# Six raw buffers for the first half slices of weights, and another order of the first loads

## The chip, the cores and the metric

The kernel runs on one core of one Trainium2 chip. The metric is the device time of one execution in microseconds; lower is better. Times of whole runs are medians; what is said of single instructions comes from one execution taken by the hardware profiler.

## What is computed

Windowed attention with block summaries, then two MLPs. For each head, a query sees the keys within 15 positions (`window` 16) and one summary per block of 32 keys: the largest key, component by component, paired with the mean of the values.

```python
k_sum = k.reshape(B, H, nb, block, D).max(axis=3)
v_sum = v.reshape(B, H, nb, block, D).mean(axis=3)
scores_l = scale * q @ k^T            # only where |i - j| < window
scores_s = scale * q @ k_sum^T + log(block)
a = softmax(concat(scores_l, scores_s))
x = a @ concat(v, v_sum)              # -> 1536 tokens x 512
h = maximum(x @ w_in1, 0); x = (h * h) @ w_out1
h = x @ w_in2; g = P(h) / (Q(h) + 1e-6); out = g @ w_out2
```

Batch 2, 8 heads, 768 positions, 64 components per head; the MLPs go from 512 to 2048 and back. The weights lie in memory as 64-bit floating point numbers; everything else is float32.

## The kernel before

The hidden dimension of the MLPs is cut into slices of 128; a slice of weights has two halves, one of `w_in` (half 0) and one of `w_out` (half 1). Half slice number k belongs to slice k // 2. Its raw 64-bit words are loaded by `w_load` (0.52 MB, lines 103 to 113) into one of three raw buffers with the tag `stage`; then three steps decode it. `w_top` (T, ScalarE, line 120) and `w_dec` (D, VectorE, lines 130 and 131) make a float32 of the two words; `w_put` (W) splits it into a high part (`wh`, ScalarE, line 144) and the rest (`wl`, GpSimd, line 145). The MLP matmuls use both: `l1` (line 532) makes the hidden values of a slice, `l2` (line 619) adds them to the output. In pass 0 the first five slices are applied to blocks of 256 tokens, between pieces of the attention that makes these tokens; passes 1 to 3 do the rest in blocks of 512.

Raw buffers come free when `w_dec` has read them. So `w_next(1)` (lines 739 to 744), the step that decodes half slice k, issues the load of half slice k + NL, where NL is the number of w loads in the list LOADS, 3. All loads go out from one queue, SP's.

The attention works on pairs d of heads and 256 queries; p is the pair of heads. In front of everything, a list LOADS gives the order of the first loads: k0 to k3 keys of a pair of heads, q0 and q1 the queries of the first 256 positions in two halves of the heads, Q1 the queries of the next 256 positions (two DMAs into `acc`), v0 to v3 values for the sums, n0 to n3 the windows of values (ten DMAs, line 318), w0 to w2 half slices. Then a list START gives, step by step, the work of the first 30 us; its instructions stay in the written order on each engine. The steps that matter here: `P`, `R` rearrange keys; `t` transposes keys (PE, line 333), `q` transposes queries (`d_t`, PE, line 397); `z` scales and spreads them (ScalarE, line 405); `s` makes the scores (PE, line 416); `m` adds the mask and finds the largest (VectorE, lines 431 and 435); `e` takes the exponential (ScalarE, line 441); `r` the sums of rows (VectorE); `n` normalises (GpSimd, line 455); `p` transposes the probabilities (PE, line 465); `b`, `f` copy them; `o` multiplies them with the values (PE, line 481); `S` adds four and four rows of the values of a pair of heads (`s_add`, GpSimd, line 286); `V` sums the rest on PE (line 373); `u` and `w` put the sums in place; `T`, `D`, `W` decode w0 to w2. The step q4 reads the queries that Q1 loads; all instructions that follow START on PE, VectorE, ScalarE and GpSimd are queued behind its last one on that engine (`tc.issue_after`), up to a point in the loop.

The work behind START is ordered by a planner that knows estimated times; the order of SP's queue behind the first loads is also its choice. `acc` (128 x 6144) is the output of pass 0, in six groups of 1024 columns, one for each block of 256 tokens; until they are written, groups 4 and 5 hold raw queries.

Of the kernel before, what the change touches and what calls it, by code (L numbers as in the profile page):

```python
# [13 lines left out]
I32 = mybir.dt.int32  # L14
# [2 lines left out]


LOADS = (
    "k0 k1 q0 k2 q1 k3 v0 v1 v3 Q1 v2 w0 n1 n0 n3 n2 w1 w2"  # L20
)
START = (
# [4 lines left out]
)  # L27
# [3 lines left out]
def tile_window_attention_moe_moe(  # L31
# [15 lines left out]
    NT, DM = out.shape  # L47
    DFF = w_in1.shape[1]
    P = 128
# [4 lines left out]
    KC = DM // P  # L54
# [11 lines left out]
    hp = ctx.enter_context(tc.tile_pool(name="hp", bufs=2))  # L66
# [7 lines left out]
    G = 2 * P  # L74
# [8 lines left out]
    acc = const.tile([P, KC * NT], F32, name="acc")  # L83
# [16 lines left out]
    wraw = {}  # L100
    wtop = [t.bitcast(I32) for t in (w_in1, w_out1, w_in2, w_out2)]

    def w_load(n, j):
        m, f = divmod(n, NF)
        r = hp.tile([P, DM, 2], I32, tag="stage", name="wraw", bufs=3)
        if j == 0:
            src = wtop[2 * m].rearrange("(k p) c -> p k c", p=P)[:, :, 2 * f * P:2 * (f + 1) * P]
            nc.sync.dma_start(out=r.rearrange("p (k f) w -> p k (f w)", k=KC), in_=src)
        else:
            nc.sync.dma_start(  # L110
                out=r.rearrange("p e w -> p (e w)"), in_=wtop[2 * m + 1][f * P:(f + 1) * P, :]
            )
        wraw[n, j] = r
# [82 lines left out]
    def build_consts():  # L196
        make_identity(nc, ident)
        for t in early[4:8]:
            nc.gpsimd.memset(t[VP:KP], 0.0)
        for z in qz:  # L200
            nc.vector.memset(z[0:D, :, 1], 0.0)
            nc.vector.memset(z[D:P, :, 0], 0.0)
        for t in prs:
            nc.vector.memset(t[:, :, HK:], 1e-9)
        m = mk[0:LO, 1, 0:WT]
        nc.vector.memset(m, 0.0)
        nc.gpsimd.affine_select(
            out=m, in_=m, pattern=[[1, WT]], compare_op=ALU.is_ge, fill=NEG, base=-1,
            channel_multiplier=-1,
        )  # L210
        nc.gpsimd.affine_select(
            out=m, in_=m, pattern=[[-1, WT]], compare_op=ALU.is_ge, fill=NEG, base=2 * WIN - 1,
            channel_multiplier=1,
        )
        nc.vector.memset(mk[:, :, WT:], math.log(BLK))
        nc.vector.tensor_copy(mk[LO:P, 1, 0:WT], m)
        m = mk[:, 1:2, 0:WT]
        nc.vector.tensor_copy(mk[:, 0:1, 0:WT], m)
        nc.vector.tensor_copy(mk[:, 2:6, 0:WT], m.to_broadcast([P, 4, WT]))
        nc.vector.memset(mk[:, 0, 0:WIN], NEG)  # L220
        nc.vector.memset(mk[:, 5, WT - WIN:WT], NEG)
        nc.gpsimd.memset(kst[VP:KP], 0.0)
        nc.vector.memset(bw, 1.0 / BLK)
        for sgn, base in ((1, 0), (-1, BLK - 1)):
            nc.gpsimd.affine_select(
                out=bw[:, WT:], in_=bw[:, WT:], pattern=[[-sgn * BLK, NB]],
                compare_op=ALU.is_ge, fill=0.0, base=base - (sgn < 0) * (TR - 1),
                channel_multiplier=sgn * TR,
            )
        nc.vector.memset(bw[:, 0:WT], 0.0)  # L230
# [23 lines left out]
    def k_rel(p, copy):  # L254

        t = early[4 + p][0:KP].rearrange("p (r h d) -> p r h d", r=TR, d=D)
        copy(out=t[0:VP].rearrange("p r h d -> p h r d"), in_=ksrc[p])
        ksrc[p] = t
# [34 lines left out]
    def q_load(g, hs=slice(0, H)):  # L293

        bb, i, _, _ = at(g * 2 * NP)
        for j in range(2):
            x = nc.sync.dma_start(
                out=qr[g % 2][:, j, hs],
                in_=q[bb, hs, (i + j) * P:(i + j + 1) * P].rearrange("h p d -> p h d"),
            )  # L300
            if g > 1:
                late(x)

    def v_load(g, hh, j):


        bb, i, _, _ = at(g * 2 * NP + j)
        t = vn[hh][j]
        t0 = i * P - WIN
        for dst, lo, n in ((t[0:WT, 0], t0, WT), (t[0:WT, 1], t0 + LO, WT)):  # L310
            segs = [(0, lo, n)]
            if lo < 0:
                segs = [(0, 0, -lo), (-lo, 0, n + lo)]
            elif lo + n > S:
                e = lo + n - S
                segs = [(0, lo, n - e), (n - e, S - e, e)]
            for r, s, m in segs:
                nc.sync.dma_start(
                    out=dst[r:r + m].rearrange("s (h d) -> s h d", d=D),
                    in_=v[bb, 4 * hh:4 * hh + 4, s:s + m, :].rearrange("h s d -> s h d"),  # L320
                )
# [16 lines left out]
    def k_lin(p, b, copy):  # L338

        pt = pk[p][b]
        src = pt[:, KE:KE + 4 * KP]
        src = bass.AP(src.tensor, src.offset, [
            list(src.ap[0]), [LO // TR, NWIN], [1, WT // TR], [KP, 4],
        ])
        dst = kt[p][:, :, 0:WT].rearrange("p w (t r) -> p w t r", r=TR)
        copy(out=dst[:, :, :, 4 * b:4 * b + 4], in_=src)
        free(pt)
# [117 lines left out]
    def d_b(d, copy=nc.scalar.copy):  # L467
        pp = ap.tile([HK, 4, 2, LO], F32, tag="pp", name="pp", bufs=2)
        copy(out=pp.rearrange("p c e t -> p (c e t)"), in_=po[d][0:HK])
        free(po[d])  # L470
        po[d] = pp
# [238 lines left out]
    v0 = {}  # L710

    def v_early(p):
# [3 lines left out]
    loads = dict(  # L716
        k=e_load, q=lambda j: q_load(0, hh[j]), Q=q_load, v=v_early,
        n=lambda i: v_load(0, *divmod(i, 2)), w=lambda i: w_load(*divmod(i, 2)),
    )
    for x in LOADS.split():  # L720
        loads[x[0]](int(x[1:]))
    NL = LOADS.count("w")
    build_consts()
    nc.gpsimd.memset(abc[:, 4:5], (1.0 + 1e-6) * 2.0 ** -62)
    nc.gpsimd.memset(abc[:, 5:6], -62.0 * math.log(2.0))
# [1 line left out]
    NW = 4 * NF  # L727
    wq = [0, 0, 0]

    def w_step(lim):  # L730

        if wq[2] < wq[1]:
            w_next(2)
        if wq[1] < wq[0]:
            w_next(1)
        if wq[0] < min(lim, NW):
            w_next(0)

    def w_next(j):
        k = wq[j]  # L740
        (w_top, w_dec, w_put)[j](*divmod(k, 2))
        wq[j] += 1
        if j == 1 and k + NL < NW:
            w_load(*divmod(k + NL, 2))

    def w_cap(ps, c, f):

# [25 lines left out]
    def v_last(h, copy):  # L773
# [5 lines left out]
        P=lambda p: k_rel(p, nc.gpsimd.tensor_copy), t=k_tr,  # L779
        l=lambda p: k_lin(p, 0, act), L=lambda p: k_lin(p, 0, dve),  # L780
        k=lambda p: k_lin(p, 1, dve), K=lambda p: k_lin(p, 1, act),
        c=lambda p: k_put(p, some, dve),
        C=lambda p: k_put(p, rest, dve, False), B=lambda p: k_put(p, rest, act, False), q=d_t, z=d_z, s=d_s, m=d_m, e=d_e,
        r=d_r, n=d_n, p=d_p, b=d_b, f=lambda d: d_b(d, dve), o=d_o, x=d_x, y=d_y,
# [5 lines left out]
    with tc.manual_schedule():  # L790
        for x in START.split():
            fn, n = parts[x[0]], int(x[1:])
# [119 lines left out]
```

## Time and profile before

| | us |
|---|---|
| median of three runs | 631.77 |
| lowest and highest run | 630.13, 632.34 |
| span of the profiled execution, first to last instruction | 629.3 |
| TensorE busy in that span | 606.4 |
| VectorE, ScalarE, GpSimd busy | 405.0, 409.8, 359.9 |

The profile gives the span of the profiled execution, not its time as a run; the median of the runs lies 2.5 us above the span. TensorE (PE) is busy for 96% of the span. PEld is the loading of its stationary operand, which runs beside the matmuls. DVE is VectorE, ACT ScalarE, POOL GpSimd, SP the engine whose queue issues the DMAs. A row of the list of instructions gives the start and the duration in us, the engine and line, the operation, what it writes and reads, a count where neighbours are merged, and in brackets how long the engine stood idle before it and what ended that.

### The profile page before, as it was taken

The numbers are of one execution on the slowest core, as the hardware profiler recorded it, in microseconds if no ns is written. First come the engines' busy times: TensorE is split into PE (matmuls) and PEld (weight loads), VectorE is DVE, ScalarE is ACT, GpSimd is POOL, SyncE is SP. The second block draws the span as 40 slices with busy tenths as digits, with TensorE's granted clock in tenths as the row PEclk, the third lists the DMA queues.
The fourth block names the chain that finished last, engine by engine and source line by source line (L and its number), as shares of the span: only waits on it lengthen the run. The fifth ranks groups of instructions, "written<-read, shape, count | busy, mean of one in ns | idle before, by whom it ended". The sixth has DMA issues, their size and how long they took to land.

```text
span 629.3 us, 9629 instructions
## 1 busy us (share of the span) xinstructions
PE 606.4 (96%) x3492; PEld 518.2 (82%) x3492; DVE 405.0 (64%) x649; ACT 409.8 (65%) x785; POOL 359.9 (57%) x367
## 2 busy tenths in 40 slices
PE   5988899999999999999999999999999999999996
PEld 5777899999998778888888888788888888888885
DVE  7977856555767642111137799987766977776672
ACT  3988767666576433122256898988878788777760
POOL 8649746435668634222276899855545765544441
PEclk9989899999999999999999999999999999999999
DMA  9989951321556530000006532410000100010011
GB/s 220 233 217 246 224 111 38 73 52 59 177 171 196 170 100 1 0 1 0 1 0 201 164 111 95 133 35 0 2 0 2 33 2 0 1 53 15 1 67 67
DMA packets 64142, 51.47 MB, mean 82 GB/s; under 512 B 39776, under 2 KB 56160, under 8 KB 64096
## 3 DMA queue, kind: packets, MB, share of 16 engines
q1 hardware_dynamic: 64096, 50.87, 29.6%
q8 instruction: 27, 0.44, 0.3%
q14 instruction: 19, 0.16, 0.1%
HBM read 47.71 MB, written 3.15 MB: 81 GB/s over the span
## 4 chain that ended last, share of the span: by engine, by line
PE 51%; DVE 7%; POOL 3%; ACT 3%; issue 1%; DVEq 0%; POOLq 0%; ACTq 0%
PE y L619 26%; PE h L532 25%; DVE wdec L131 2%; POOL wl L145 2%; ACT wdec L120 1%; POOL sl L596 1%; DVE h L581 1%; DVE wdec L130 1%; DVE q L578 1%; DVE p L566 1%; DVE p L584 1%; DVE acc L645 1%; DVE p L565 1%; ACT sh L595 1%; ACT wh L144 0%
## 5 line engine op out<-in xcount | busy, mean ns | idle before, releaser
L532 PE MATMUL h<-xh,wh 128*128 128x512 f32 (+1 forms) x444 | 162.5, 366 | 3.7 <-DVE r L562 2.3
L532 PE MATMUL h<-xh,wl 128*128 128x512 f32 (+1 forms) x444 | 161.1, 364 | 2.1 <-POOL wl L145 2.1
L532 PE MATMUL h<-xl,wh 128*128 128x512 f32 (+1 forms) x444 | 161.3, 364 | 0.0
L596 POOL TENSOR_TENSOR sl<-r,sh 128x512 fp32r<-128x512 f32 (+1 forms) x63 | 69.1, 1097 | 105.6 <-ACT sh L595 92.4
L553 POOL TENSOR_TENSOR q<-q,u 128x512 f32<-128x512 f32 x48 | 63.7, 1327 | 76.2 <-ACT q L550 73.2
L145 POOL TENSOR_TENSOR wl<-wdec,wh 128x512 fp32r<-128x512 f32 x64 | 87.2, 1374 | 22.1 <-ACT wh L144 22.1
L532 PEld LDWEIGHTS h<-xh,wh 128*128 128x128 f32 x444 | 84.4, 190 | 17.6 <-DVE r L562 2.5
L532 PEld LDWEIGHTS h<-xh,wl 128*128 128x128 f32 x444 | 84.4, 190 | 15.2 <-POOL wl L145 2.7
L532 PEld LDWEIGHTS h<-xl,wh 128*128 128x128 f32 x444 | 84.6, 191 | 12.5
L562 DVE TENSOR_TENSOR r<-r,h 128x512 f32<-128x512 f32 (+1 forms) x63 | 34.9, 556 | 88.9 <-ACT r L545 88.8
L619 PE MATMUL y<-sh,wh 128*128 128x512 f32 (+1 forms) x252 | 86.1, 345 | 1.2 <-ACT sh L595 1.2
L619 PE MATMUL y<-sh,wl 128*128 128x512 f32 (+1 forms) x252 | 84.7, 339 | 0.0
L619 PE MATMUL y<-sl,wh 128*128 128x512 f32 (+1 forms) x252 | 78.6, 342 | 0.3 <-POOL sl L596 0.3
L596 POOL TENSOR_TENSOR sl<-p,sh 128x512 fp32r<-128x512 f32 x48 | 65.0, 1355 | 20.4 <-ACT sh L595 16.5
L619 PE MATMUL y<-wl,sh 128*128 128x512 f32 x192 | 74.7, 389 | 0.0
L619 PE MATMUL y<-wh,sh 128*128 128x512 f32 x192 | 74.4, 389 | 0.0
L619 PE MATMUL y<-wh,sl 128*128 128x512 f32 x192 | 73.6, 389 | 0.0
L131 DVE SCALAR_TENSOR_TENSOR wdec<-wraw,wdec 128x512 int32<-128x512 int32 x64 | 67.9, 1061 | 1.4
L130 DVE TENSOR_SCALAR wdec<-wdec 128x512 int32<-128x512 int32 x64 | 44.8, 700 | 22.2 <-ACT wdec L120 22.0
L595 ACT CAST sh<-r 128x512 fp32r<-128x512 f32 (+1 forms) x63 | 32.4, 514 | 39.5 <-PE y L619 38.6
L144 ACT CAST wh<-wdec 128x512 fp32r<-128x512 f32 x64 | 39.3, 621 | 28.8 <-DVE wdec L131 26.9
L545 ACT ACTIVATE r<-h 128x512 f32<-128x512 f32 (+1 forms) x63 | 31.0, 493 | 41.3 <-PE h L532 23.6
(94 smaller groups left out, 1106.8 us busy)
## 6 DMA issues: line engine op xcount, KB each, us to landing
wraw<-in_moe_w_in_dram SPq DMA_DIRECT2D x32, 512.0 KB, 4.1
wraw<-in_moe_w_out_dram SPq DMA_DIRECT2D x32, 512.0 KB, 3.4
early<-in_v_dram SPq DMA_DIRECT2D x40, 96.0 KB, 3.3
out_dram<-acc SPq DMA_DIRECT2D x12, 256.0 KB, 2.1
acc<-in_q_dram SPq DMA_DIRECT2D x10, 256.0 KB, 6.1
early<-in_k_dram SPq DMA_DIRECT2D x4, 384.0 KB, 5.4
early<-in_v_dram SPq DMA_DIRECT2D x4, 384.0 KB, 8.6
kst<-in_k_dram SPq DMA_DIRECT2D x8, 192.0 KB, 6.2
```

Source lines behind the costliest of these rows:

```text
L120: x = nc.scalar.activation(out=f32(t), in_=f32(r[:, :, 1]), func=AF.Prelu, scale=2.0 ** -112, alpha=-(2.0 ** 32))
L130: nc.vector.tensor_single_scalar(out=t, in_=t, scalar=3, op=ALU.logical_shift_left)
L131: nc.vector.scalar_tensor_tensor(out=t, in0=low, scalar=29, in1=t, op0=ALU.logical_shift_right, op1=ALU.bitwise_or)
L144: nc.scalar.copy(out=th[:, j], in_=t)
L145: nc.gpsimd.tensor_tensor(out=tl[:, j], in0=t, in1=f32(th[:, j]), op=ALU.subtract)
L532: nc.tensor.matmul(hq[g][:, 0:n], lhsT=w[:, 0, ws], rhs=x[:, part, ts], start=(part == 0 and j == 0), stop=(part == KC - 1 and j == 2),)
L545: nc.scalar.activation(out=r, in_=h, func=AF.Relu)
L553: nc.gpsimd.tensor_tensor(out=q_, in0=q_, in1=u_, op=ALU.mult)
L562: nc.vector.tensor_tensor(out=eq[g], in0=eq[g], in1=h, op=ALU.mult)
L595: nc.scalar.copy(out=sh[:, 0:n], in_=e)
L596: nc.gpsimd.tensor_tensor(out=sl[:, 0:n], in0=e, in1=f32(sh[:, 0:n]), op=ALU.subtract)
L619: nc.tensor.matmul(o, lhsT=lt, rhs=rt, start=(f == 0 and j == 0 and d * m % 512 == 0), stop=(f == FS[ps] - 1 and j == 2 and (d + 1) * m % ...
```

## The change

The first six half slices of weights are loaded before START instead of three. w0 to w2 go to the three `stage` buffers as before; w3 to w5 go to groups 1 to 3 of `acc`, taken as integers. The step that decodes half slice 0, 1 or 2 issues the load of number 6, 7 or 8; the one that decodes 3, 4 or 5 issues none; from 6 on it issues the third next, as before. In LOADS, the queries Q1 go from the place after v3 to the place after w1, and w3, w4 and w5 are added behind w2. In START, the sum S2 goes from behind p1 to the place behind S3.

```diff
 LOADS = (
-    "k0 k1 q0 k2 q1 k3 v0 v1 v3 Q1 v2 w0 n1 n0 n3 n2 w1 w2"
+    "k0 k1 q0 k2 q1 k3 v0 v1 v3 v2 w0 n1 n0 n3 n2 w1 Q1 w2 w3 w4 w5"
 )
 START = (
...
-    "t3 c2 X2 r0 s2 m1 K3 S1 l3 m2 c3 e1 r1 e2 n0 V0 S3 p0 f0 n1 q4 s3 r2 u0 p1 S2 z4 s4 B1 "
+    "t3 c2 X2 r0 s2 m1 K3 S1 l3 m2 c3 e1 r1 e2 n0 V0 S3 S2 p0 f0 n1 q4 s3 r2 u0 p1 z4 s4 B1 "
...
     def w_load(n, j):
         m, f = divmod(n, NF)
-        r = hp.tile([P, DM, 2], I32, tag="stage", name="wraw", bufs=3)
+        k = 2 * n + j
+        if 3 <= k < NL:
+            r = acc[:, (k - 2) * KC * G:(k - 1) * KC * G].bitcast(I32)
+            r = r.rearrange("p (e w) -> p e w", w=2)
+        else:
+            r = hp.tile([P, DM, 2], I32, tag="stage", name="wraw", bufs=3)
...
+    NL = LOADS.count("w")
     for x in LOADS.split():
         loads[x[0]](int(x[1:]))
-    NL = LOADS.count("w")
...
         wq[j] += 1
-        if j == 1 and k + NL < NW:
-            w_load(*divmod(k + NL, 2))
+        if j == 1 and not 3 <= k < NL:
+            k += NL if k < 3 else 3
+            if k < NW:
+                w_load(*divmod(k, 2))
```

## Rows read from the trace of the kernel before

**Rows 1.** The table of stretches: us, busy time by engine, granted clock, DMA.

```profile
core 0: us, PE busy (x) PEld busy (x) DVE busy (x) ACT busy (x) POOL busy (x), PEclk, DMA share, GB/s
...
32.00:36.00 4.00, 2.94 (x24) 2.52 (x22) 3.48 (x7) 2.54 (x6) 1.91 (x2) 1.00 1.23 213
36.00:44.00 8.00, 7.17 (x58) 6.88 (x59) 5.10 (x12) 7.25 (x20) 4.62 (x7) 0.79 0.78 236
44.00:60.00 16.00, 13.19 (x114) 10.54 (x115) 12.30 (x30) 14.13 (x38) 12.30 (x18) 1.00 0.99 216
...
68.00:76.00 8.00, 5.70 (x35) 5.49 (x36) 7.84 (x15) 4.72 (x15) 4.29 (x5) 0.79 0.89 212
76.00:200.00 124.00, 123.50 (x1114) 116.58 (x1113) 76.38 (x145) 83.27 (x210) 70.88 (x107) 1.00 0.39 107
```

**Rows 2.** The chain that ended last: shares of the span by engine.

```profile
PE 51%; DVE 7%; POOL 3%; ACT 3%; issue 1%; DVEq 0%; POOLq 0%; ACTq 0%
```

**Rows 3.** The list of instructions, SP alone: issues of Q1, w1 and w4.

```profile
7.35 1.77 SPq L297 DMA_DIRECT2D acc<-in_q_dram  x2
...
22.95 0.48 SPq L110 DMA_DIRECT2D wraw<-in_moe_w_out_dram  x1
...
36.35 0.42 SPq L108 DMA_DIRECT2D wraw<-in_moe_w_in_dram  x1
```

**Rows 4.** The view of DMA from 3 to 27 us: busy tenths, amount.

```profile
DMA  9999999999999999999999999999999999996966
...
DMA packets 9727, 5.88 MB, mean 245 GB/s; under 512 B 7583, under 2 KB 8188, under 8 KB 9726
```

**Rows 5.** Line 297 from 7 to 9 us: the two DMAs of Q1.

```profile
L297 SPq DMA_DIRECT2D acc<-in_q_dram x2: 387/419/451, 7.3 to 8.7; - x2
...
DMA to landing us min/median/max: 9.8/9.8/9.8
```

**Rows 6.** Line 110 from 22 to 24 us: the load w1.

```profile
DMA to landing us min/median/max: 5.0/5.0/5.0
```

**Rows 7.** The list of instructions, PE: steps q4, s3, s4.

```profile
20.39 0.38 PE L397 MATMUL pt<-ident,acc 128*128 128x128 f32 x2
21.12 1.12 PE L416 MATMUL pss<-kt,qz 128*128 128x120 f32 x8 [0.35 <-DVE kt L361]
...
23.53 1.06 PE L416 MATMUL pss<-kt,qz 128*128 128x120 f32 x8
```

**Rows 8.** The list of instructions: steps z4, m3 and S2.

```profile
22.13 0.78 ACT L405 ACTIVATE qz<-pt 64x256 f32<-64x256 f32 x2
...
23.09 0.63 DVE L431 TENSOR_TENSOR pr<-pss,mask 128x480 f32<-128x480 f32 x1
...
23.28 1.28 POOL L286 TENSOR_TENSOR early<-early 96x512 f32<-96x512 f32 x1
```

**Rows 9.** The list of instructions, PE: scores after a drop of the clock.

```profile
38.69 1.90 PE L416 MATMUL pss<-kt,qz 128*128 128x120 f32 x8
```

**Rows 10.** The list of instructions: waits for weights and for normalised rows.

```profile
36.83 0.19 PEld L532 LDWEIGHTS h<-xh,wl 128*128 128x128 f32 x1 [1.41 <-POOL wl L145]
...
41.27 0.69 ACT L120 ACTIVATE wdec<-wraw 128x512 f32<-128x512 f32 x1 [0.62 <-DMA wraw<-in_moe_w_in_dram]
...
46.89 0.19 PEld L532 LDWEIGHTS h<-xh,wh 128*128 128x128 f32 x1 [0.68 <-ACT wh L144]
...
49.47 0.19 PEld L532 LDWEIGHTS h<-xh,wl 128*128 128x128 f32 x1 [1.10 <-POOL wl L145]
...
52.95 0.14 PEld L465 LDWEIGHTS ptp<-ident,pr 128*120 128x120 f32 x1 [0.89 <-POOL pr L455]
```

**Rows 11.** The list of instructions: the wait at 71.8 us and what precedes it.

```profile
62.76 5.63 POOL L286 TENSOR_TENSOR vst<-vst 96x512 f32<-96x512 f32 x6
...
68.11 2.75 DVE L131 SCALAR_TENSOR_TENSOR wdec<-wraw,wdec 128x512 int32<-128x512 int32 x1
...
71.81 0.29 PEld L532 LDWEIGHTS h<-xh,wh 128*128 128x128 f32 x1 [2.51 <-DVE r L562]
```

## The prediction

> **What bounds the kernel now.** I read three views first. The table of stretches [rows 1] says where TensorE stands still: from 76 us on it is busy 123.50 of 124.00 us, so whatever time is won or lost earlier is carried to the end unchanged. What can move lies before 76 us. There it is idle 4.00 - 2.94 = 1.06 us in 32 to 36, 8.00 - 7.17 = 0.83 in 36 to 44, 16.00 - 13.19 = 2.81 in 44 to 60 and 8.00 - 5.70 = 2.30 in 68 to 76, together 7.0 us; and the granted clock is 0.79 in two of these stretches, which costs 2 x 8 x 0.21 = 3.4 us if TensorE had work all the while. So 10.4 us is all that earlier weights could give back. The chain that ended last [rows 2] holds little but matmuls; it is no guide to the first 76 us, which it doesn't reach. The second view is SP's list of issues [rows 3] beside the load on the DMA engines [rows 4]: SP has one queue, it issues in the order of LOADS, and from 3 to 27 us all 16 engines are busy and move 245 GB/s, to the last two slices. In that stretch a load lands when what stands ahead of it has been moved. The third is the order of TensorE in START [rows 7], for each step of START stands on its engine in the written order.
>
> **The change, part by part.**
>
> *Q1 behind w1.* This is the load of queries for d=4 to 7. Before, it is issued at 7.35 us and lands 9.8 us later [rows 3, 5], its second half at about 18.5. The step q4 transposes it on TensorE at 20.39 [rows 7]: some 2 us of slack. The change puts v2, w0, the ten n loads and w1 ahead of it, and leaves q4 where it stands in START. What must then be moved up to the end of Q1 is, piece for piece, what must be moved before up to the end of w1 (4 k, 2 q, 4 v, Q1, w0, 4 n, w1). w1 is issued at 22.95 and lands 5.0 us later [rows 3, 6], at 27.95; since the engines are full all that time, I put Q1's landing there. From below: everything up to w2 is moved by about 27 us [rows 4]; without w2's 0.52 MB, 2.1 us at 245 GB/s, it is moved by 24.9, and if nothing came between moving and landing, that is the earliest. From above: one more load of that size ahead of it would take 0.52 MB / 245 GB/s = 2.1 us, so 30.0.
>
> So TensorE, which takes its instructions in order, stands at q4 from about 20.4 to 28.0: 7.6 us (4.5 to 9.6). Queued behind q4 on TensorE are s3, p1, s4, V1 and o0. On ScalarE z4 waits for q4, and behind it B1, w0, b1, e3 and T0; on VectorE m3 waits for s3, and behind it C3, m4, r3 and D0; GpSimd runs dry after n2. Hardly anything can be done in the meantime, because all that follows START on these engines is tied behind its last instruction.
>
> How much of it comes through: z4 starts at 22.13 before, because ScalarE was not free sooner, and m3 at 23.09 [rows 8]. Afterwards q4 ends at 28.0 + 0.4, z4 starts there (6.3 later than before); s3 takes 1.1 us more [rows 7], and m3 starts at about 29.6 (6.5 later). The dense rest of START follows m3 and z4 on ScalarE and VectorE, so I carry 6.5 us (3.4 to 8.5 with the landing).
>
> *The clock after the wait.* TensorE would be idle 7.6 us. After the idle time at 68 to 72 the granted clock is 0.79 on the mean of 68 to 76 [rows 1], a mixture of the two levels, 2.4 and 1.2 GHz. The eight score matmuls take 1.06 us at the upper level and 1.90 after a drop [rows 7, 9]. s3, ahead of m3, would be 0.8 us longer, and q4 0.2: I add 1.0 us (0, if the clock holds, to 1.9, with s4 too).
>
> *w3, w4 and w5 before START, into acc.* The three raw half slices take groups 1 to 3 of acc, which pass 0 writes only when its second block of tokens is done, long after they are decoded. So the wait for the buffer goes. No instruction is added; the loads that followed D0, D1 and D2 are now w6 to w8, three half slices further on, and from w9 on the distance is three again. SP's queue gets three loads of 0.52 MB, 6.4 us at 245 GB/s, ahead of the value loads for the next pair of tiles; these can't start before o0 to o3 have run, by then the queue has drained, and I cost them at nothing (if they are late, o4 waits, at most the 6.4 us). What it gives: before, w4 is issued at 36.35, held by the value loads ahead of it on SP [rows 3]; ScalarE waits for it at 41.27 and TensorE stands at 46.89 and 49.47 for the halves of the weights made from it, 0.68 and 1.10 us [rows 10]. Those 1.8 us go. At 52.95 it waits 0.89 for the normalised rows that GpSimd made behind two weight subtractions; earlier weights would spread these, and I count half, 0.5. The wait of 1.41 at 36.83 hangs on W2 [rows 10], which is in START and needs no new load: it stays, and so does the clock drop behind it.
>
> At 71.81 TensorE waits 2.51 for VectorE, which was in one weight decode of 2.75 us while GpSimd added values for 5.63 us and then had a weight subtraction [rows 11]. It waits, and the clock drop behind it is 8 x 0.21 = 1.7. With weights ahead of need that decode may fall elsewhere, or another in its place: half of 2.3 + 1.7, so 2.0. The Trainium skill ("SBUF — State Buffer", section "SBUF: two separate sides") says that a GpSimd instruction and a VectorE instruction with two SBUF inputs lock each other out for a whole instruction. By that rule the price follows the two orders and not the loads, and 4.0 us or nothing would be counted instead of 2.0; this row agrees with a lockout, but no row shows where the pair falls after the change.
>
> Together 1.8 + 0.5 + 2.0 = 4.3 us back (0, if each wait only gives way to another, to 10.4, all that TensorE loses).
>
> *S2 before n1, v2 earlier.* S2 took 1.28 us at 23.28 [rows 8]; the new place is before n1, in a gap of GpSimd, so n2 can start that much earlier. It gains nothing while m3 and r3 are late by 6.5; without the late Q1 it would be worth at most its 1.3 us and at worst delays n1 by as much if v2 were late (it now lands sooner). I take 0.
>
> **The sum.** Against the profiled execution of 629.3 us span: +6.5 + 1.0 + 0 - 4.3 = +3.2, a span of 632.5. The median of the runs is 631.77, 2.5 above that span; I add the 3.2 to the median: 635.0.
>
> **The rivals.**
>
> *A, forecast: the late Q1 costs more than the early weights give.* 635.0; its own range from 633.7 to 640.0, that is +1.9 to +8.2, the upper end with a landing at 30 and little back. For it: an order of queues that can be read row by row. Chance 0.58, and 0.02 beyond 640.
>
> *B, they cancel.* The wait at q4 is there, but some 7.5 of the 10.4 us come back: 631.8, within 0.3%. For it: the START part of the waits (36.83 and its clock drop) may also shift when everything moves. Against: those are not made by loads. 0.18.
>
> *C, Q1 isn't late.* If Q1 lands by 20.4 after all, because loads pass each other in the queue or SP keeps another order than LOADS, the 7.5 us fall away and the 4.3 remain: 627.5. Against: landings before follow the order of issue, Q1 before w1 by 9 us. The Trainium skill ("DMA: Bandwidth & Descriptors", section "Queues, rings and completion order") states that completions need not come in order of issue, though each engine takes its descriptors in ring order; the landings here are in order. 0.10.
>
> *D, the other side: the weights, and not START, set the pace up to 76 us.* The delay of START is time in which w3 to w5 land and DMA traffic drains; decoding then runs ahead, all 10.4 us come back and 7.5 are paid: -2.9, so 628.9. It decides from the point where more than 7.5 of the 10.4 come back, nearly three quarters. Against: ScalarE is busy 14.13 of 16.00 us in 44 to 60 [rows 1], so it has little room to decode ahead. 0.12.
>
> **How the numbers follow.** About 0.3%, 1.9 us, is what a measurement of this kernel can tell from no change. Slower is A and beyond: 0.60; the same is B: 0.18; faster is C and D: 0.22. The range must reach past B to D: from 628.5 to 640.5 it leaves out C (0.10), a part of D (0.05) and what lies beyond 640 (0.02).
>
> **What would show it.** In the profile after, TensorE's q4 (line 397 of before) should start near 28 us instead of 20.39, released by the load of q, with an idle time of 6 to 9 us ahead of it, and the first matmuls of line 532 about 7 us later than before. Q1's issue on SP should stand behind w1's. The wait of ScalarE for w4 should be gone, and so TensorE's two waits for weights made from it. If q4 starts by 22 us the first term is wrong, and with it the sign. If q4 is late and the time isn't longer, the recovery was mis-sized, and the stretch in which TensorE is idle less than before will say where.

## The result and the profile after

| | before | after | forecast |
|---|---|---|---|
| median of the runs, us | 631.43 | 635.57 | 635.0 |
| ratio, 95% interval | | 1.0068 [1.0048, 1.0089] | 1.005 |
| span of the profiled execution, us | 629.3 | 633.8 | 632.5 |

The changed kernel is slower by 4.1 us (the ratio gives 0.0068 x 631.43 = 4.3). Lines of the new kernel stand 5 below those of the old one: q4 is line 402 (397), the scores 421 (416), `l1` 537 (532), `l2` 624 (619).

First SP's issues, which answer [rows 3]: start, duration, line, what is loaded.

```profile
9.60 11.11 SPq L323 DMA_DIRECT2D early<-in_v_dram  x10
20.75 0.48 SPq L115 DMA_DIRECT2D wraw<-in_moe_w_out_dram  x1
21.27 1.06 SPq L302 DMA_DIRECT2D acc<-in_q_dram  x2
22.37 3.07 SPq L113 DMA_DIRECT2D wraw<-in_moe_w_in_dram  x1
...
26.51 0.50 SPq L115 DMA_DIRECT2D acc<-in_moe_w_out_dram  x1
```

The ten value loads hold SP for 11.11 us; Q1 (third line) goes out at 21.27 instead of 7.35, and w5, the last of the six half slices, at 26.51. TensorE's list shows what q4, s3 and s4 then did, beside [rows 7], and when `l1` began:

```profile
26.88 0.45 PE L402 MATMUL pt<-ident,acc 128*128 128x128 f32 x1 [6.22 <-DMA acc<-in_q_dram]
27.62 0.48 PE L402 MATMUL pt<-ident,acc 128*128 128x128 f32 x1 [0.30 <-DMA acc<-in_q_dram]
27.89 1.90 PE L421 MATMUL pss<-kt,qz 128*128 128x120 f32 x8
...
30.44 1.22 PE L421 MATMUL pss<-kt,qz 128*128 128x120 f32 x8
...
38.73 0.36 PE L537 MATMUL h<-xh,wh 128*128 128x256 f32 x1
```

Before, the first matmul of `l1` stood here:

```profile
31.89 0.36 PE L532 MATMUL h<-xh,wh 128*128 128x256 f32 x1
```

q4 waits 6.22 + 0.30 = 6.5 us for the load (in brackets: the idle time and what ended it), s3 behind it runs at 1.90 us instead of 1.12, and the first matmul of `l1` starts at 38.73 instead of 31.89: 6.8 us late. ScalarE's row for z4 says the same, against 22.13 in [rows 8]:

```profile
28.20 0.78 ACT L410 ACTIVATE qz<-pt 64x256 f32<-64x256 f32 x2 [5.98 <-PE pt L402]
```

The table of stretches, with the columns of [rows 1]:

```profile
20.00:28.00 8.00, 1.49 (x10) 0.98 (x9) 3.66 (x7) 2.19 (x8) 4.33 (x10) 0.75 1.02 224
...
44.00:60.00 16.00, 13.10 (x125) 11.79 (x124) 14.23 (x30) 15.13 (x40) 10.24 (x17) 0.89 0.69 163
...
68.00:76.00 8.00, 6.12 (x50) 5.78 (x48) 7.85 (x12) 5.38 (x13) 7.88 (x10) 0.79 0.96 182
76.00:200.00 124.00, 124.00 (x1139) 118.26 (x1139) 79.38 (x153) 85.25 (x216) 72.35 (x112) 1.00 0.40 112
```

From 20 to 28 us TensorE is busy 1.49 of 8.00 us at a mean granted clock of 0.75, a mixture of 1.2 and 2.4 GHz. From 76 to 200 us it is busy 124.00 of 124.00 us, so what is late there is still late at 200. Before, 0.50 us are missing from the 124: a wait for GpSimd's value sums, which is gone after the change.

```profile
95.31 0.48 PE L373 MATMUL pvs<-vst,bw 96*120 96x128 f32 x2 [0.50 <-POOL vst L286]
```

Between 36 and 76 us its list shows these waits of 0.3 us and more, which stand against [rows 10] and the last row of [rows 11]:

```profile
41.96 0.39 PE L537 MATMUL h<-xh,wh 128*128 128x256 f32 x1 [0.69 <-ACT wh L149]
...
43.67 0.38 PE L537 MATMUL h<-xh,wl 128*128 128x256 f32 x1 [1.20 <-POOL wl L150]
...
51.66 0.69 PE L486 MATMUL pav<-pp,early 120*64 120x64 f32 x16 [1.12 <-ACT pr L446]
...
58.40 0.38 PE L624 MATMUL y<-sh,wh 128*128 128x256 f32 x1 [1.77 <-ACT sh L600]
...
60.65 0.39 PE L624 MATMUL y<-sl,wh 128*128 128x256 f32 x1 [0.32 <-POOL sl L601]
...
71.37 0.39 PE L624 MATMUL y<-sl,wh 128*128 128x256 f32 x1 [1.84 <-POOL sl L601]
```

The two at 42 and 44 hang on W2, as the one at 36.83 did before. None is left for the weights of w4, none for normalised rows, and the wait for VectorE at 71.81 is gone. Four others have come: for the exponential (1.12), and three for the two parts of the squared hidden values (1.77, 0.32, 1.84). The last of them hangs on a load: GpSimd stands still 3.23 us for the values that it has to sum, which it didn't before [rows 11], and the part that TensorE waits for (start 70.59, 0.72 us) is queued behind the first two of these sums.

```profile
68.12 2.52 POOL L291 TENSOR_TENSOR vst<-vst 96x512 f32<-96x512 f32 x2 [3.23 <-DMA vst<-in_v_dram]
```

ScalarE no longer waits for w4; its decode T4 finds the load landed, but starts 5.3 us later than the 41.27 of [rows 10]:

```profile
46.61 0.66 ACT L125 ACTIVATE wdec<-acc 128x512 f32<-128x512 f32 x1
```

So START is 6.8 us late, and w4 isn't decoded sooner than before.

How late the kernel is further on can be read from the chain of waits, here the same run of `l2` matmuls in each kernel, before and then after. Ahead of it each kernel has 1,730 records of matmuls, as many of every form in the one as in the other, so the same work has been done by then.

```profile
223.39 3.08 PE y L619 x12
```

```profile
227.84 3.07 PE y L624 x12
```

It is 4.45 us late there, as it is at the end (633.8 - 629.3 = 4.5). Of the 6.8 us some 2.4 have come back between START and there.

### The profile page after: what moved, and what is told of

It is laid out like the page before. It is cut to its first block, busy times and chain, and to the rows that moved or that the text cites. A ratio compares the mean times of both kernels' runs of the same rounds, so it can differ in the third digit from the quotient of the medians.

```text
span 633.8 us, 9626 instructions
## 1 busy us (share of the span) xinstructions
PE 605.4 (96%) x3492; PEld 519.6 (82%) x3492; DVE 407.3 (64%) x649; ACT 410.6 (65%) x785; POOL 359.0 (57%) x367
## 4 chain that ended last, share of the span: by engine, by line
PE 50%; DVE 7%; POOL 2%; ACT 2%; issue 1%; DMA 1%; DVEq 0%; POOLq 0%; ACTq 0%; SPq 0%
PE y L624 26%; PE h L537 25%; DVE wdec L136 2%; POOL wl L150 1%; POOL sl L601 1%; ACT wdec L125 1%; DVE h L586 1%; DVE q L583 1%; DVE wdec L135 1%; DVE p L571 1%; DVE p L589 1%; DVE acc L650 1%; DVE p L570 1%; DMA wraw<-in_moe_w_out_dram 1%; ACT sh L600 1%
## 5 line engine op out<-in xcount | busy, mean ns | idle before, releaser
L136 DVE SCALAR_TENSOR_TENSOR wdec<-wraw,wdec 128x512 int32<-128x512 int32 x61 | 66.0, 1083 | 1.4
```

The costliest lines, as they stand in the source:

```text
L136: nc.vector.scalar_tensor_tensor(out=t, in0=low, scalar=29, in1=t, op0=ALU.logical_shift_right, op1=ALU.bitwise_or)
```

## The experiments

Three theories were put against each other. T, that of the forecast: the late Q1 costs more than the whole change does, the early weights give a part of it back, and the two are independent. R1: the late Q1 costs nothing by itself, and what costs is the new order of the work behind START; Q1 alone would then give the time of before. R2: the late Q1 is the whole of it and the early weights give nothing; Q1 alone would then give the time of after.

**Q1 late, alone.** Before, with one load moved; every engine but SP has the instructions of before in the order of before.

```diff
-    "k0 k1 q0 k2 q1 k3 v0 v1 v3 Q1 v2 w0 n1 n0 n3 n2 w1 w2"
+    "k0 k1 q0 k2 q1 k3 v0 v1 v3 v2 w0 n1 n0 n3 n2 w1 Q1 w2"
```

> The kernel before with one edit: Q1 goes behind w1 in the list of loads; three raw buffers and the old order of the sums stay. On every engine but SP's queue the order of instructions is that of the kernel before. Theory T (the late Q1 costs the 6.9 us by which the rest of START is late in the profile after, and the early weights give some 2.7 us back): 631.4 + 6.9 = 638.3, TensorE idle 6 to 7 us ahead of q4. Rival R1 (the wait at q4 is made up later, what costs is the three extra loads or the planner's new order): 631.4. Rival R2 (of the 6.9 us slack takes up 2.8 whatever the weights do, and the early weights are worth nothing): 635.5.

Measured: 639.38 us beside 632.1, ratio 1.0105 [1.0075, 1.0134], that is +6.6 us (4.7 to 8.5). TensorE's list at q4:

```profile
27.48 0.45 PE L397 MATMUL pt<-ident,acc 128*128 128x128 f32 x1 [6.95 <-DMA acc<-in_q_dram]
```

One load moved costs 6.6 us by itself. R1 falls, which wanted 1.000. R2 wanted the 1.0068 of after, which lies below this interval, but after's own interval reaches into it (to 1.0089); the next two kernels decide on R2. (The profiled execution, 640.72 us, is the slowest of its runs; its trace, with the first `l1` at 40.04, 8.15 us late, shows the upper end.)

**Q1 back, the rest as after.** The instructions of after in their order, but for SP.

```diff
-    "k0 k1 q0 k2 q1 k3 v0 v1 v3 v2 w0 n1 n0 n3 n2 w1 Q1 w2 w3 w4 w5"
+    "k0 k1 q0 k2 q1 k3 v0 v1 v3 Q1 v2 w0 n1 n0 n3 n2 w1 w2 w3 w4 w5"
```

> The changed kernel with one edit: Q1 goes back to its place behind v3 in the list of loads; six raw buffers and the new order of the sums stay. On every engine but SP's queue the order of instructions is that of the changed kernel. T: no wait at q4 and the gain of the early weights remains, 631.4 - 2.7 = 628.7. R1: still 635.5. R2: 631.4.

Measured: 629.16 beside 632.1, ratio 0.9957 [0.9939, 0.9975]. TensorE has no wait at q4; s3 waits for a copy of keys, and START ends 0.8 us late, which is made up by the end (span 627.3):

```profile
20.75 0.38 PE L402 MATMUL pt<-ident,acc 128*128 128x128 f32 x2
22.06 1.12 PE L421 MATMUL pss<-kt,qz 128*128 128x120 f32 x8 [0.92 <-DVE kt L366]
```

The order of the engines that after has is, without the late Q1, faster than before. It isn't the new order that costs, and R2, which wanted 1.000 here, falls as well.

**Six buffers alone.** Before, with the buffers and w3 to w5; Q1 and S2 in their old places.

```diff
-    "k0 k1 q0 k2 q1 k3 v0 v1 v3 Q1 v2 w0 n1 n0 n3 n2 w1 w2"
+    "k0 k1 q0 k2 q1 k3 v0 v1 v3 Q1 v2 w0 n1 n0 n3 n2 w1 w2 w3 w4 w5"
```

> The kernel before with six raw buffers and w3, w4 and w5 behind w2 in the list of loads; Q1 and S2 keep their places. Beside the run with Q1 put back it differs in S2's place alone. If S2's place is worth nothing, as I took it, both have one time (T 628.7, R1 635.5, R2 631.4); if GpSimd's earlier second normalisation reaches TensorE, this one is up to 1.3 us slower than that one.

Measured: 629.02 beside 632.1, ratio 0.9953 [0.9933, 0.9972], so -3.0 us (1.8 to 4.2). From the kernel above it differs by the place of S2 alone, and the two agree within 0.2 us: S2's place is worth nothing that can be told here (each is known to about 1.2 us). The two parts add up: (0.0105 - 0.0047) x 632.1 = +3.7 against +4.3 for the change. The traces add up too. Behind START, TensorE has the same order here as in after; START ends at 31.86 here, 6.87 us sooner than in after, and the run of `l2` matmuls starts 6.57 us sooner:

```profile
221.27 3.07 PE y L624 x12
```

So nearly the whole delay of START arrives there, and what came back of the 6.8 us is what six buffers give without a late Q1: 223.39 - 221.27 = 2.1. But TensorE's waits behind START are these:

```profile
44.77 0.69 PE L486 MATMUL pav<-pp,early 120*64 120x64 f32 x16 [1.09 <-ACT pr L446]
51.50 0.39 PE L624 MATMUL y<-sh,wh 128*128 128x256 f32 x1 [1.77 <-ACT sh L600]
...
64.95 0.58 PE L624 MATMUL y<-sl,wh 128*128 128x256 f32 x1 [2.32 <-POOL sl L601]
```

The waits for w4's weights are gone, and waits of 1.09, 1.77, 0.32 and 2.32 us have come. They are the four of after (1.12, 1.77, 0.32, 1.84) some 7 us earlier, so the late Q1 isn't what makes them; GpSimd's wait for the values to be summed is here too (3.47 us, till 61.46). Nor is it the order alone: with Q1 back, TensorE has the same order and waits 0.88, 1.30, 0.80, 0.66 and 1.52 us there, and the time is the same. Before, the waits of [rows 10, 11] from 46 us on are some 0.2 shorter at the matmuls than at the weight loads (0.50, 0.91, 0.70, 2.31); with two of 0.20 and 0.40 for ScalarE they came to 5.0 us there; the new ones come to 1.09 + 1.77 + 0.32 + 2.32 = 5.5, no less, and yet the run of `l2` is 2.1 us earlier.

The waits at the matmuls are not the whole, though: a wait of the weight load ahead of a matmul (PEld) can lie under the record of the matmul before it, as one of 0.26 us for normalised rows does at 51.92 in before. The view of waits adds up what the weight loads waited for; here are two of its rows for before, from 31.8 to 223.3 us, and two for after, from 38.7 to 227.8 (waited for, us in total, times, longest):

```profile
PEld h L532 <- DVE r L562: 2.5, 1, 2.5
PEld ptp L465 <- POOL pr L455: 1.8, 5, 0.9
```

```profile
PEld y L624 <- POOL sl L601: 2.7, 3, 2.0
PEld ptp L470 <- POOL pr L460: 0.4, 2, 0.2
```

| from the first `l1` to the run of `l2` | before | six buffers alone | after |
|---|---|---|---|
| length, us | 191.50 | 189.41 | 189.11 |
| waits of weight loads, all rows, us | 12.5 | 10.5 | 10.1 |
| waits of matmuls, all rows, us | 7.9 | 7.5 | 7.2 |
| mean granted clock | 0.98 | 0.98 | 0.98 |

By the weight loads six buffers save 2.0 us and after saves 2.4, and the stretch is shorter by 2.1 and 2.4, at the same clock. That is what comes back.

**Four buffers, and five.** The same with fewer early half slices.

```diff
-    "... v0 v1 v3 Q1 v2 w0 n1 n0 n3 n2 w1 w2 w3 w4 w5"
+    "... v0 v1 v3 Q1 v2 w0 n1 n0 n3 n2 w1 w2 w3"       # four
+    "... v0 v1 v3 Q1 v2 w0 n1 n0 n3 n2 w1 w2 w3 w4"    # five
```

> The kernel before with one more raw buffer: w3 is loaded before START, w4 after D0 and w5 after D1. w4 then goes out where w3 did, at 28.6, and lands some 8 us before ScalarE comes to it: 629.0, if w4's wait is all that the early loads remove; 631.4 - 1/3 x 2.4 = 630.6, if each load gives its share.

> The kernel before with two more raw buffers and not three: w3 and w4 are loaded before START, w5 after D0. If what the early loads give is that w4 lands before ScalarE comes to it, the time is that of six buffers, 629.0. If each load before START gives its share, 631.4 - 2/3 x 2.4 = 629.8. If the planner's order, which differs again, decides, anything from 628 to 633.

Measured: four 630.65 beside 631.66, ratio 0.9995 [0.9978, 1.0012]; five 631.81, ratio 1.0008 [0.9991, 1.0025]. In both, ScalarE doesn't wait for w4, and T4 starts at 40.16 and 40.17 instead of 41.27. TensorE's waits of 0.50 and 0.91 for W4's halves have shrunk to one, in four and in five:

```profile
47.19 0.39 PE L537 MATMUL h<-xh,wl 128*128 128x256 f32 x1 [0.24 <-POOL wl L150]
```

```profile
47.57 0.38 PE L537 MATMUL h<-xh,wl 128*128 128x256 f32 x1 [0.39 <-POOL wl L150]
70.79 0.44 PE L402 MATMUL pt<-ident,acc 128*128 128x128 f32 x2 [1.67 <-DVE xl L505]
```

So the removal of nearly all of the waits that the forecast priced at 1.8 us gives nothing that can be measured: the gain of 1.8 (-0.0028) lies outside both intervals. In five a wait of 1.67 stands at 70.79 where 2.31 stood at 71.81. In four the wait for GpSimd's value sums, 0.50 at 95.31 before, has grown, where six buffers and after have none:

```profile
94.81 0.48 PE L378 MATMUL pvs<-vst,bw 96*120 96x128 f32 x2 [1.77 <-POOL vst L291]
```

Counted at the weight loads as above, the waits behind START come to 13.2 us with four and 11.8 with five, against 12.5 before (the mean granted clock there is 0.99 and 0.98).

**Seven buffers.** w6 early as well, with groups 0 to 3 of `acc`.

```diff
-    "... w1 w2 w3 w4 w5"
+    "... w1 w2 w3 w4 w5 w6"
-            r = acc[:, (k - 2) * KC * G:(k - 1) * KC * G].bitcast(I32)
+            r = acc[:, (k - 3) * KC * G:(k - 2) * KC * G].bitcast(I32)
```

> The kernel with six raw buffers and Q1 and S2 in their old places, and a seventh: w6 is loaded before START too, into group 3 of acc, w3 to w5 into groups 0 to 2. If earlier landing is what helps, no more than with six: 629.0, or slightly less. If the planner's order decides, which is another again: 628 to 633, as for four and five buffers (630.7 and 631.8).

Measured: 635.31 beside 630.29, ratio 1.0068 [1.0046, 1.009]. Loads behind the seventh come too late:

```profile
40.98 0.34 PE L486 MATMUL pav<-pp,early 120*64 120x64 f32 x4 [0.96 <-DMA early<-in_v_dram]
...
44.12 0.47 PE L402 MATMUL pt<-ident,acc 128*128 128x128 f32 x1 [0.84 <-DMA acc<-in_q_dram]
```

With six, TensorE has no such wait there; the seventh pushes values and queries of the next tiles past their use. These waits, 1.8 us, aren't the whole of the 6 to 7 us by which seven is above six: behind them the granted clock is 0.65 in 44 to 52 us and 0.79 in 52 to 60, and the planner's order is another one again.

**Three loads that nobody reads, ahead of w3.** From six buffers alone: d0 to d2 load 2.1 MB into buffers that are written again later. If six buffers gain because weights land early, the gain should go when they land late in the same order.

```diff
-    "... w1 w2 w3 w4 w5"
+    "... w1 w2 d0 d1 d2 w3 w4 w5"
```

> The kernel with six raw buffers and Q1 and S2 in their old places, and three loads without a reader (2.1 MB, into places that are written again later) between w2 and w3 in the list of loads. At 245 GB/s w3 to w5 land 8.6 us later, w4 near 41.5, where it landed before the change, and the value loads behind them as well. The order of instructions on every engine is that of the kernel without them, apart from matmuls in the last passes. If the gain of 2.4 to 3.0 us comes from w3 to w5 landing sooner, it is gone: 631.4 or more, with ScalarE waiting for w4. If it comes from the order that the planner chose, 629.0, and up to 2 us more for the late value loads.

Measured: 639.47 beside 630.29, ratio 1.013 [1.0099, 1.0161]. ScalarE and TensorE:

```profile
41.61 0.66 ACT L125 ACTIVATE wdec<-acc 128x512 f32<-128x512 f32 x1 [4.26 <-DMA acc<-in_moe_w_out_dram]
```

```profile
47.84 1.01 PE L486 MATMUL pav<-pp,early 120*64 120x64 f32 x12 [2.00 <-DMA early<-in_v_dram]
```

The order of six buffers, with its loads late, is slower than before: the order alone doesn't give the gain. More isn't settled: what came late was w3, which was on time in before as well, and the values, not w4 and w5 alone.

**Q1 behind w0.** After, with Q1 past v2 and w0 only.

```diff
-    "... v0 v1 v3 v2 w0 n1 n0 n3 n2 w1 Q1 w2 w3 w4 w5"
+    "... v0 v1 v3 v2 w0 Q1 n1 n0 n3 n2 w1 w2 w3 w4 w5"
```

> The changed kernel with Q1 behind w0 instead of w1; on every engine but SP's queue the order of instructions is that of the changed kernel. What is moved up to the end of Q1 is then what was moved up to the end of w0 before, which landed at 21.6 us. T by its own rule: TensorE waits 1 to 2 us at q4, but ScalarE is not free for z4 before 22.1, so START is late by 0.5 and not by 6.9: 629.1 + 0.5 = 629.6. If any wait at q4 counts in full: 630.6. If the place of Q1 costs through something else than its landing (SP's queue, the n loads behind it): 632 or more.

Measured: 629.25 beside 630.29, ratio 0.9989 [0.9971, 1.0006]; by its trace 2.7 us faster (span 626.6, but with a granted clock of 1.00 all along, where before has 0.79 in two stretches). q4's wait:

```profile
20.75 0.27 PE L402 MATMUL pt<-ident,acc 128*128 128x128 f32 x1
21.84 0.33 PE L402 MATMUL pt<-ident,acc 128*128 128x128 f32 x1 [0.82 <-DMA acc<-in_q_dram]
```

Up to the end of START the 0.82 us cost nothing: ScalarE starts z4 at 22.50 and the first `l1` starts at 32.65, against 22.50 and 32.67 with Q1 in its old place and no wait. So a wait comes through there less a slack, as the forecast had it. In the time it is not shown: the medians are 629.25 and 629.16, but beside before, measured together with each, the ratios are 0.9989 and 0.9957, 2.0 us apart, and the forecast of the rival, that any wait counts in full, isn't excluded.

**q4 later in START.** The loads of after; q4 and all that hangs on it moved behind n3. If the price is only the place of q4 in TensorE's queue, it should go.

```diff
-    "... n1 q4 s3 r2 u0 p1 z4 s4 B1 w0 m3 V1 n2 C3 o0 m4 p2 b1 e3 T0 r3 D0 n3 e4 r4 n4 o1 ..."
+    "... n1 s3 r2 u0 p1 B1 w0 m3 V1 n2 C3 o0 p2 b1 e3 T0 r3 D0 n3 q4 z4 s4 m4 e4 r4 n4 o1 ..."
```

> The changed kernel with its order of loads, Q1 behind w1, but q4, z4, s4, m4, e4, r4 and n4 stand behind n3 in START, so that TensorE reaches q4 some 6 us later. T (what costs is not the late load as such but that q4 stands ahead of work that doesn't need it): the wait at q4 shrinks to under 1 us and the time comes to that of the kernel with Q1 put back, 629.1, or up to 1.5 us more, as ScalarE gets e4 later. Rival (the late Q1 delays what follows START as well, as d=4 is the first of the next pair of tiles): 632 or more.

Measured: 634.57 beside 631.66, ratio 1.0047 [1.003, 1.0064]. The wait at q4 is 1.42 us, but ScalarE and TensorE wait elsewhere (lines 3 above those of after):

```profile
29.56 0.78 ACT L407 ACTIVATE qz<-pt 64x256 f32<-64x256 f32 x2 [2.28 <-PE pt L399]
33.03 1.25 ACT L443 ACTIVATE pr<-pr,mx 128x120 f32<-128x120 f32 x4 [2.68 <-DVE mx L437]
```

```profile
35.93 1.98 PE L483 MATMUL pav<-pp,early 120*64 120x64 f32 x32 [1.86 <-ACT wh L146]
```

The chain from Q1 to q4, z4, s4, m4 and e4 now has little beside it; the granted clock is 0.72 in 28 to 36 us, and the first `l1` starts at 39.56, later than in after, though the time, 634.57, isn't above after's 635.57 (the intervals overlap). The sharp form of T, that only q4's place matters, falls: what is late is the whole chain behind Q1, and in this place too queues stand still for it.

**TensorE kept at work during the wait.** After, with 90 or 29 matmuls of the identity, read by nobody, ahead of q4 and in the bank that q4 overwrites.

```diff
-    "... n0 V0 S3 S2 p0 f0 n1 q4 s3 ..."
+    "... n0 V0 S3 S2 p0 f0 n1 X29 q4 s3 ..."    # or X90
+        if n > 2:
+            banks.insert(0, banks.pop())
```

> The changed kernel with 90 small matmuls of the identity ahead of q4 on TensorE, in the bank that q4 takes next, so that TensorE works while it waits for Q1. If the clock drop after the wait costs the 1.0 us that the prediction adds, 635.6 - 1.0 = 634.6 and the score matmuls of s3 take about 1.1 us and not 1.9. If START is paced by ScalarE and VectorE there whatever the clock, 635.6. If the matmuls outlast Q1's landing, up to 1 us more.

> The changed kernel with 29 matmuls of the identity ahead of q4 in place of the 90 tried before, which took 20.3 us (two passes each, 0.113 us a pass) and outlasted the load by 13 us. 29 take 6.5 us at the upper clock and end near 27.0, Q1 lands at 26.9 to 27.6. In the run with 90 the stretch from q4 to the first matmul of line 537 was 10.1 us, in the changed kernel 11.9, of which 0.7 is the second half of Q1 landing later: if the clock makes the rest, this run has s3 at about 1.1 us, the first matmul of line 537 at 37.6 and not 38.7, and a time 1.1 us shorter, 634.5. If ScalarE and VectorE pace that stretch, 635.6.

With 90 the size was wrong: each such matmul is two records of 0.113 us, and they ran far past Q1's landing.

```profile
20.40 20.26 PE L773 MATMUL warm<-ident 128*128 128x128 f32 x180
```

647.05 us beside 632.1, ratio 1.0238 [1.021, 1.0267], by medians 11.5 us more than after. q4 starts at 40.72, 13.8 later than in after, and from q4 to the first `l1` it took 10.07 us instead of 11.85, 1.8 less (0.7 of it since both halves of Q1 are there at once); 13.8 - 1.8 = 12.0. A delay of q4 comes through nearly whole. With 29 the fillers end when Q1 has landed:

```profile
20.75 6.64 PE L773 MATMUL warm<-ident 128*128 128x128 f32 x58
27.45 0.79 PE L402 MATMUL pt<-ident,acc 128*128 128x128 f32 x2
28.08 1.06 PE L421 MATMUL pss<-kt,qz 128*128 128x120 f32 x8
```

s3 takes 1.06 us instead of 1.90 and the first `l1` starts at 37.89, 0.84 earlier. The time is 634.55 beside 631.66, ratio 1.0056 [1.0037, 1.0076]; that is 1.0 us below after, by medians, and the intervals overlap. By START's end the clock's share is 0.8 us; that the total has it is not shown.

## Why the prediction was right, and where its sizes were off

*Q1's landing.* Right, and by the reason given: a load lands when what stands ahead of it has been moved. Forecast 28.0, measured 27.6 for the second half (q4's second transpose starts there) and 26.9 for the first, which alone releases the first transpose. The wait was 6.5 us instead of 7.6. Rival C, that Q1 is there by 20.4, falls with it. (The engines' row in [rows 4] is below nine tenths in three of its last four slices, so they are full up to about 24.6 us and not to the last two slices; the landing didn't hang on that.)

*What comes through.* Forecast 6.5 + 1.0 = 7.5 at the end of START; measured 6.8 there, and +6.6 (4.7 to 8.5) in the time with Q1 alone. Of the 6.8, 6.0 remain when the fillers keep the clock up (37.89 - 31.89), against the 6.5 forecast. That a wait comes through less a slack is seen with Q1 behind w0, at the end of START. That what is late at 76 us is late at the end is borne out: of the 6.87 us between six buffers alone and after, 6.57 are left at the run of `l2`.

*The clock.* Forecast 0.8 for s3 and 0.2 for q4; s3 took 0.84 more than with fillers, and START ended 0.84 later. Right in size at START's end.

*S2.* Forecast 0; measured 629.16 and 629.02 with and without its move, no difference that can be told.

*The recovery: the step that failed, in its items.* Forecast 4.3; six buffers alone give 3.0 (1.8 to 4.2), and 2.4 came back in the trace of after. So this term was too large by 1.3 to 1.9 us, and the START term by 0.7 to 0.9; they have opposite signs, and that the sum, +3.2, came so near the +4.1 to 4.3 measured owes something to luck. The items of the recovery are not what happened either. The 1.8 us for W4's waits are nearly gone with four and with five buffers too, and these gain nothing. The 0.5 for normalised rows was too small: at the weight loads these waits went from 1.8 to 0.4 us. And the sum put at nothing the waits that would come in their place, 1.12, 1.77, 0.32 and 1.84 us. Its lower bound, that each wait only gives way to another, comes closer: TensorE's waits from 46 to 76 us that went make 0.50 + 0.91 + 0.70 + 0.20 + 0.40 + 2.31 = 5.0 us at the matmuls, those that came 1.12 + 1.77 + 0.32 + 1.84 = 5.05. It isn't the whole either: at the weight loads, counted up to the run of `l2`, the waits fell by 2.4, as much as came back. So the gain is the difference of waits that went and waits that came, and not the sum of those that the early weights remove. Six early half slices, with the order that the planner makes of them, leave less waiting than four or five with theirs. Which part of the order gives it, and whether the early landing of w4 and w5 is needed for it, stays open: the loads that nobody reads delayed other things as well.

The forecast also took it that whatever is won before 76 us is carried to the end unchanged. With four buffers it isn't: the wait of 1.77 at 94.81 lies behind that.

*VectorE's long decode.* Half of 4.0 us was counted, since no row showed where the pair of VectorE and GpSimd would fall. The pair recurs:

```profile
72.62 2.95 DVE L136 SCALAR_TENSOR_TENSOR wdec<-wraw,wdec 128x512 int32<-128x512 int32 x1
```

```profile
71.28 2.08 POOL L291 TENSOR_TENSOR vst<-vst 96x256 f32<-96x256 f32 x3
73.33 1.27 POOL L150 TENSOR_TENSOR wl<-wdec,wh 128x512 fp32r<-128x512 f32 x1
74.56 0.45 POOL L291 TENSOR_TENSOR vst<-vst 96x128 f32<-96x128 f32 x1
```

The decode takes 2.95 us, against a median of 0.90 for this line, while GpSimd goes from one sum to the next until 75.0. The Trainium skill ("SBUF — State Buffer", section "SBUF: two separate sides") says that the two lock each other out for whole instructions; this row agrees. TensorE doesn't wait for this decode, but for GpSimd (1.84 at 71.37), which was late with the value sums because their load was late (3.23). The granted clock of 68 to 76 us is 0.79 as before: of the 4.0 us of which half was counted, the wait of 2.3 gave way to one of 1.84, and the drop of the clock stayed.

*The rivals.* B, that the recovery pays for the late Q1, asked 7.5 us of it; it gave 2.4 in this trace and 3.0 alone. D, that decoding would run ahead during START's delay, is refuted by T4, which starts 5.3 us later than before; ScalarE was busy 15.13 of 16.00 us in 44 to 60. What beats both kernels is the change without its late Q1: six buffers with Q1 in its old place, 629.02 us, 0.9953 of before.

## What to carry to other kernels

In a queue that issues in order, a load that moves back lands with its new neighbours; subtract from that landing the place of its first reader, and what is left over, less the slack of the next engine in its chain, is the price. Moving the reader back didn't save it here, since the whole chain hangs on it. Earlier loads that only take a short wait away can gain nothing (four and five buffers), and one load too many ahead of others can cost more than its wait (seven). Where waits are traded for waits, don't add up only those that go, nor idle time at the matmuls alone: count the waits at the weight loads too, look behind the stretch in question, and compare when the same piece of work starts in both kernels, further down.

## What the runs showed of the hardware

- The issue itself can hold a queue: ten DMAs of values held SP for 11.11 us in after, while w1 right behind them took 0.48. A load's place in the list is then also its time of issue.
- A 128 x 128 float32 matmul of the identity is two records of 0.113 us at a granted clock of 1.00: 29 fill 6.64 us.
